# A float64 piece's conversion in the empty places of a weight tile's scale chain

## The chip, the cores and the metric

One core of a Trainium2 chip runs the kernel. The metric is the device time of one execution in microseconds, lower is better; it is given as the median of several runs.

## The reference

Attention with a sliding window of 128 keys and a distance bias gives x (2304 tokens, 512 wide). A mixture of experts follows: `P` comes from eight rounds of row and column normalisation of `exp(x @ w_gate)`, and the output is the sum over eight experts. A last block has a leaky ReLU:

```python
for e in range(E):                       # E = 8, D = 512, F = 1024
    h = np.maximum(x @ w1[e], 0.0)
    out += P[:, e:e + 1] * (h @ w2[e])
...
h = x @ w_in                             # 512 x 2048, float64 here
g = np.maximum(0.01 * h, h)
return (g @ w_out).astype(np.float32)    # 2048 x 512, float64 here
```

`w_in` and `w_out` arrive as float64; all other inputs are float32.

## The kernel before

After the attention the two feed-forward blocks are worked through in 20 **chunks** of 512 hidden columns: 16 for the experts (two for each), four for the last block. A chunk has a first weight tile (512 x 512 of `w1` or `w_in`) and a second one (512 x 512 of `w2` or `w_out`). The tokens stand in five groups, `PAIRS` 0 to 4, of four or two tiles of 128; a **unit** is one chunk with one group, and from chunk 1 on the units of a chunk run in the order 0, 4, 1, 2, 3.

The 2 x 2 block products are formed with seven multiplications (`PRODUCTS`), each on operands split into two float16 halves, so that a product of 256 columns takes six matmuls. `a_steps` makes the seven products of the first multiplication for a unit (line 727), `b_steps` those of the second (line 844). A group of tokens with two halves has 14 a steps and 14 b steps, group 4 has 7 and 7; 126 steps make a chunk. Every product is taken out of PSUM by ACT or DVE before a later one adds to the same bank: a steps by ACT (L739, at the seventh product L751) or DVE (L743), b steps by DVE (L857) or by ACT and POOL (L854, L855). `later` hangs the ReLU, the split of h and its sums (L775, L781, L797 on ACT, L756 on DVE, L800 on POOL) some steps behind. `merge` weaves a unit's a steps with the b steps of the unit before.

Beside this runs the preparation of the next chunk's weights, in the list `side`. At unit 4 of a chunk `side_jobs` fills it; every step ends with a tick that takes the next one or two places of the list, a place being a job or `None`, an empty place. `Weights.load` brings 1 MB to a buffer `raw` (L571, on SP's queue). `Weights.scale` has four squares with a row sum (`largest`, L575, ACT), the eight places of `scale_jobs` (`one` L413 and L415 on DVE; `two` a matmul L421 and small DVE steps L423 to L434; `three` a matmul L440 and a copy L441; the other five are empty), then four scalings (L578, ACT). `early` has two splits (L446 on ACT, L447 on POOL) and four sums (L602, POOL); the other splits come with the last steps of the chunk, and only then is `raw` free. `W[0]` are the first weights (`a` in `side_jobs`), `W[1]` the second (`b`).

`to_single` turns a piece of 256 KB of `w_in` or `w_out` into float32 in DRAM. Its load (L650, 512 KB, SP) goes to a buffer `raw` too, and its five jobs are `exponent` (L656 on DVE, L659 on ACT), `signed` (L662, DVE), `high` (L667 on DVE, L668 on ACT), `low` (L674 on ACT, L676 on POOL) and `put` (L680 on POOL, then the store L681 on SP's queue). There are 32 pieces; chunks 1 to 10 convert three each, chunk 11 two, later ones none. `raw` has two buffers, so in a chunk with three pieces the first weights follow the first piece in one buffer, and the third piece and then the second weights follow the second piece in the other: each of these loads waits for the store of the piece whose buffer it takes, and SP's queue is in order.

What sets the order on each engine: the program is traced in the order in which the jobs are written, and `TileContext(nc, schedule_with_timeline_sim=True)` (L1100) orders each engine's queue when the kernel is compiled, from modelled times; of two instructions that it takes for ready the one written first goes first. `pop` ties every instruction of a job behind the last step instruction (`anchor`) of the same engine, and behind nothing else. So a place in the list is the earliest point of a job in its engine's queue.

Of the kernel before, what the change touches and what calls it, by code (L numbers as in the profile page):

```python
# [31 lines left out]
def attn_moe_kernel(  # L32
# [19 lines left out]
    KT = DM // P  # L52
# [577 lines left out]
    def weights(ci):  # L630
        for which in range(2):
            W[which][ci] = Weights(ci, which)
# [367 lines left out]
    def side_jobs(ci, n):  # L1000

        todo = [to_single(cast.pop(0)) for _ in range(min(n, len(cast)))]
        weights(ci)
        a, b = W[0][ci], W[1][ci]
        jobs = [load for load, _ in todo[:2]]
        if not todo:
            return [a.load, b.load] + [None] * 10 + a.scale() + a.early() + b.scale() + b.early()
        jobs += [None] * 8 + todo[0][1] + [a.load]
        if len(todo) > 1:
            jobs += todo[1][1]  # L1010
        if len(todo) > 2:
            jobs += [todo[2][0]] + [None] * 4 + a.scale() + todo[2][1] + [b.load] + a.early()
        else:
            jobs += [b.load] + [None] * 8 + a.scale() + a.early()
        return jobs + [None] * 8 + b.scale() + b.early()

    def weigh(ci):
        pu[ci] = small.tile([P, NTILE], F32, tag="pu", name="pu")
# [12 lines left out]
    for n, u in enumerate(units + [None]):  # L1031
        a, b = [], b_steps(*prev)
        if u is not None:
            ci, p = u
            assert ci < NCE or p in split_pairs
            a = a_steps(ci, p)
            k0 = len(a) - 7
            if p == ends[ci] and ci + 1 < NC:
                a = [[f] + ([lambda j=k - k0: W[0][ci + 1].at(j)] if k >= k0 else []) for k, f in enumerate(a)]
            else:  # L1040
                a = [[f] for f in a]
        if prev[1] == ends[prev[0]] and prev[0] + 1 < NC:
            k0 = len(b) - 7
            b = [[f] + ([lambda j=k - k0: W[1][prev[0] + 1].at(j)] if k >= k0 else []) for k, f in enumerate(b)]
        else:
            b = [[f] for f in b]
        if u is not None and ci >= 1:
            if n and units[n - 1][0] != ci and ci != NCE:
                weigh(ci)
            if p == 4:  # L1050
                side += side_jobs(ci + 1, 3 if ci < NCE - 1 else 0) if ci + 1 < NC else []
# [65 lines left out]
```

## Time and profile before

| | us |
|---|---|
| median of 3 runs | 1922.75 |
| lowest and highest of them | 1921.96, 1922.90 |
| the profiled execution | 1919.44 |
| its span, first to last instruction | 1917.6 |

| engine | busy us | share of the span |
|---|---|---|
| PE | 1846.7 | 96% |
| ACT | 1363.5 | 71% |
| POOL | 1325.3 | 69% |
| DVE | 1309.4 | 68% |

The profile is one execution on the core. Times are microseconds from the first instruction, unless ns is written. PE is TensorE's matmuls, DVE VectorE, ACT ScalarE, POOL GpSimd, SP the engine that issues all transfers; SPq marks an issue on its queue. L575 is line 575 of the kernel. An instruction is named by line, operation, and its tiles as out<-in. A row of a timeline has start, duration, engine, line, operation, tiles, shape, count, and in brackets the time for which the engine sat idle before it with what ended that idle time.

### The profile page before, as it was taken

What the parts mean: (1) busy time and instruction counts of PE and PEld (TensorE: products, weight loads), DVE (VectorE), ACT (ScalarE), POOL (GpSimd) and SP (SyncE); (2) the same over time, 40 slices, a digit from 0 to 9 for tenths busy, and PEclk for the clock granted to TensorE, in tenths of its full rate; (3) what the DMA queues carried; (4) which work ended last, traced back from release to release, by engine and by line L of the source; (5) the groups of instructions that cost most, each with busy time, mean ns of one, the idle gap of its engine ahead of it and who ended that gap; (6) DMA issues with size and microseconds to landing.
All of it is one profiled execution on the core that took longest, in us unless ns stands there. A gap on an engine that the chain in (4) does not pass through costs nothing.

```text
span 1917.6 us, 45101 instructions
## 1 busy us (share of the span) xinstructions
PE 1846.7 (96%) x17725; PEld 1606.4 (84%) x17725; DVE 1309.4 (68%) x3606; ACT 1363.5 (71%) x3125; POOL 1325.3 (69%) x1142
## 2 busy tenths in 40 slices
PE   7899889999999999999999999999999998999998
PEld 4677777888888888988888898988989787888897
DVE  5456567767676777767676777666666787677776
ACT  7978767776767677676676667666666779776764
POOL 3843566777868687877868687675767786665753
PEclk9999999999999999999999999999999999999999
DMA  7522002112111202111111201100001010101001
GB/s 231 171 89 84 2 19 77 33 63 64 43 57 39 84 24 72 51 45 67 40 62 34 84 23 56 45 23 23 23 24 45 1 46 1 45 2 45 2 29 72
DMA packets 57861, 97.80 MB, mean 51 GB/s; under 512 B 3632, under 2 KB 22064, under 8 KB 57648
## 3 DMA queue, kind: packets, MB, share of 16 engines
q1 hardware_dynamic: 57648, 94.92, 15.1%
q8 instruction: 138, 2.26, 0.5%
q14 instruction: 75, 0.61, 0.1%
HBM read 81.81 MB, written 13.11 MB: 49 GB/s over the span
## 4 chain that ended last, share of the span: by engine, by line
PE 76%; ACT 8%; DMA 5%; POOL 4%; DVE 4%; issue 2%; SPq 0%; POOLq 0%; ACTq 0%; DVEq 0%
PE t L844 36%; PE s L727 21%; PE sq L727 15%; DMA raw<-in_moe_w_dram 4%; ACT junk L575 2%; ACT e L261 1%; PE o L305 1%; DVE s L756 1%; POOL h L800 1%; PE pt L288 1%; PE s L249 1%; POOL w L447 1%; ACT xp L446 1%; ACT raw L578 1%; ACT pb L292 1%
## 5 line engine op out<-in xcount | busy, mean ns | idle before, releaser
L844 PE MATMUL t<-w,h 128*128 128x256 f16 x7560 | 978.7, 273 | 17.7 <-DVE acc L857 6.2
L727 PEld LDWEIGHTS <-w 128*128 128x128 f16 x8400 | 758.4, 98 | 110.4 <-issue 28.7
L844 PEld LDWEIGHTS <-h 128*128 128x128 f16 x7560 | 729.2, 98 | 114.5 <-issue 27.2
L727 PE MATMUL s<-xp,w 128*128 128x256 f16 (+1 forms) x4872 | 610.9, 262 | 18.5 <-ACT q L751 11.6
L857 DVE SCALAR_TENSOR_TENSOR acc<-t,pu,acc 128x256 f32<-128x256 f32 x864 | 407.2, 478 | 213.5 <-PE t L844 162.6
L800 POOL TENSOR_TENSOR h<-s,h 128x1024 f16<-128x1024 f32 x180 | 388.5, 2158 | 122.7 <-ACT h L797 81.8
L727 PE MATMUL sq<-xp,w 128*128 128x256 f16 (+1 forms) x3528 | 451.9, 262 | 3.0 <-DVE s L756 2.6
L855 POOL TENSOR_TENSOR acc<-acc,part 128x256 f32<-128x256 f32 x324 | 235.5, 729 | 283.1 <-ACT part L854 252.9
L447 POOL TENSOR_TENSOR w<-raw,w 128x512 f16<-128x512 f32 x240 | 277.8, 1167 | 45.9 <-ACT w L446 45.5
L756 DVE SCALAR_TENSOR_TENSOR h<-sq,h 128x512 f16<-128x512 f32 (+1 forms) x352 | 192.4, 551 | 84.2 <-ACT h L781 49.4
L854 ACT ACTIVATE part<-t,pu 128x256 f32<-128x256 f32 x324 | 152.6, 471 | 110.0 <-PE t L844 101.7
L797 ACT ACTIVATE h<-s 128x1024 f16<-128x1024 f32 x180 | 189.7, 1054 | 43.2 <-DVE s L756 41.7
L743 DVE SCALAR_TENSOR_TENSOR sq<-sq,q 128x256 f32<-128x256 f32 x352 | 150.0, 427 | 62.5 <-PE sq L727 54.8
L739 ACT ACTIVATE q<-s 128x256 f32<-128x256 f32 x364 | 137.8, 380 | 71.7 <-PE s L727 59.1
L446 ACT ACTIVATE w<-raw 128x512 f16<-128x512 f32 x240 | 148.2, 628 | 8.4 <-PE t L844 6.0
L756 DVE SCALAR_TENSOR_TENSOR s<-sq,s 128x256 f32<-128x256 f32 x352 | 145.9, 414 | 2.1
L775 ACT ACTIVATE h<-sq 128x512 f16<-128x512 f32 x176 | 104.4, 593 | 55.4 <-PE t L844 30.4
L756 DVE SCALAR_TENSOR_TENSOR s<-sq,q 128x256 f32<-128x256 f32 x352 | 131.4, 414 | 13.5 <-ACT q L751 11.7
L743 DVE SCALAR_TENSOR_TENSOR sq<-s,q 128x256 f32<-128x256 f32 x176 | 75.3, 428 | 84.0 <-ACT q L739 78.9
L575 ACT ACTIVATE junk<-raw 128x512 bf16<-128x512 f32 x160 | 100.2, 627 | 44.8 <-DMA raw<-in_moe_w_dram 43.6
L781 ACT ACTIVATE h<-sq 128x256 f16<-128x256 f32 x176 | 66.7, 379 | 65.0 <-DVE sq L743 58.2
L578 ACT ACTIVATE raw<-raw,sr 128x512 f32<-128x512 f32 x160 | 102.4, 716 | 2.3 <-DVE sr L441 1.9
(142 smaller groups left out, 1702.6 us busy)
## 6 DMA issues: line engine op xcount, KB each, us to landing
raw<-in_moe_w_dram SPq DMA_DIRECT2D x32, 1024.0 KB, 5.2
k_t<-in_k_dram SPq DMA_DIRECT2D x16, 512.0 KB, 4.0
raw<-in_moe_w_in_dram SPq DMA_DIRECT2D x16, 512.0 KB, 3.6
raw<-in_moe_w_out_dram SPq DMA_DIRECT2D x16, 512.0 KB, 3.5
q_t<-in_q_dram SPq DMA_DIRECT2D x18, 256.0 KB, 4.1
v_t<-in_v_dram SPq DMA_DIRECT2D x18, 256.0 KB, 2.7
acc<-in_v_dram SPq DMA_DIRECT2D x18, 256.0 KB, 6.0
out_dram<-acc SPq DMA_DIRECT2D x18, 256.0 KB, 2.0
```

The costliest lines, as they stand in the source:

```text
L446: nc.scalar.activation(out=hi, in_=src, func=AF.Copy)
L447: return nc.gpsimd.tensor_tensor(out=lo, in0=src, in1=hi, op=ALU.subtract)
L575: nc.scalar.activation(out=junk, in_=self.raw[:, k], func=AF.Square, accum_out=self.mx[:, k:k + 1])
L727: nc.tensor.matmul(d[b][:, f, :], t[:, wp, kk, ft * P:(ft + 1) * P], XP[p][:, o, kk, xp, :], start=(i == 0 and f == 0 and j in FIRST), sto ...
L743: nc.vector.scalar_tensor_tensor(out=block(k), in0=ps, scalar=CS, in1=q[:, k], op0=ALU.mult, op1=ALU.add)
L756: nc.vector.scalar_tensor_tensor(out=out, in0=in0, scalar=sc, in1=in1, op0=op0, op1=op)
L797: nc.scalar.activation(out=h[:, 3:7, 0, :], in_=d["s"], func=AF.Copy)
L800: nc.gpsimd.tensor_tensor(out=h[:, 3:7, 1, :], in0=d["s"], in1=h[:, 3:7, 0, :], op=ALU.subtract)
L844: nc.tensor.matmul(ps, h[:, o, hp, f, tt * P:(tt + 1) * P], w[:, wp, ft, :], start=(i == 0 and j in FIRST), stop=(i == 5), skip_group_chec ...
L854: nc.scalar.activation(out=part, in_=ps, func=AF.Copy, scale=s)
L855: nc.gpsimd.tensor_tensor(out=dst, in0=dst, in1=part, op=ALU.add)
L857: nc.vector.scalar_tensor_tensor(out=dst, in0=ps, scalar=s, in1=dst, op0=ALU.mult, op1=ALU.add)
```

## The change

It alters `side_jobs` where three pieces are converted. The first weights' squares move eight places back, so that 18 places lie between their load and the first of them. The third piece's five conversion jobs leave their places behind the scalings and take the five empty places of the first weights' scale chain. The second weights' load moves one place forward, the first weights' scalings nine back (behind that load), and `early` three back; three empty places less stand ahead of the second weights' squares, which keep their place. The list keeps its 85 places. With two pieces or none the list is the same as before.

```diff
         jobs = [load for load, _ in todo[:2]]
         if not todo:
             return [a.load, b.load] + [None] * 10 + a.scale() + a.early() + b.scale() + b.early()
+        scale = a.scale()
         jobs += [None] * 8 + todo[0][1] + [a.load]
         if len(todo) > 1:
             jobs += todo[1][1]
         if len(todo) > 2:
-            jobs += [todo[2][0]] + [None] * 4 + a.scale() + todo[2][1] + [b.load] + a.early()
+            load, cast_jobs = todo[2]
+            cast_jobs = list(cast_jobs)
+            chain = [cast_jobs.pop(0) if job is None and cast_jobs else job for job in scale[KT:KT + 8]]
+            jobs += [load] + [None] * 12 + scale[:KT] + chain + cast_jobs + [b.load] + scale[KT + 8:] + a.early() + [None] * 5
         else:
-            jobs += [b.load] + [None] * 8 + a.scale() + a.early()
-        return jobs + [None] * 8 + b.scale() + b.early()
+            jobs += [b.load] + [None] * 8 + scale + a.early() + [None] * 8
+        return jobs + b.scale() + b.early()
```

Places of the list of 85, counted from 0:

| job | before | after |
|---|---|---|
| first weights' load | 15 | 15 |
| second piece's five jobs | 16 to 20 | 16 to 20 |
| third piece's load | 21 | 21 |
| first weights' squares | 26 to 29 | 34 to 37 |
| `one`, `two`, `three` | 30, 33, 36 | 38, 41, 44 |
| `exponent`, `signed`, `high`, `low`, `put` | 42, 43, 44, 45, 46 | 39, 40, 42, 43, 45 |
| second weights' load | 47 | 46 |
| first weights' scalings | 38 to 41 | 47 to 50 |
| first weights' splits and sums | 48 to 53 | 51 to 56 |
| second weights' squares | 62 to 65 | 62 to 65 |

## Rows read from the trace of the kernel before

**Rows 1.** The page's head: span, and busy time of each engine

```profile
span 1917.6 us, 45101 instructions
PE 1846.7 (96%) x17725; PEld 1606.4 (84%) x17725; DVE 1309.4 (68%) x3606; ACT 1363.5 (71%) x3125; POOL 1325.3 (69%) x1142
```

**Rows 2.** Busy time by stretch: PE, PEld, DVE, ACT, POOL, PEclk, DMA; chunks 9, 14

```profile
941.40:1026.60 85.20, 84.04 (x804) 74.49 (x803) 60.50 (x155) 59.89 (x130) 65.55 (x56) 1.00 0.16 54
1347.00:1430.60 83.60, 83.60 (x804) 74.62 (x803) 54.20 (x146) 54.45 (x121) 57.32 (x49) 1.00 0.08 27
```

**Rows 3.** Who waited for whom: us in total, times, longest us

```profile
ACT junk L575 <- DMA raw<-in_moe_w_dram: 43.6, 22, 2.8
...
PE s L727 <- ACT q L751: 11.6, 13, 1.5
```

**Rows 4.** Timeline of ACT in chunk 9, around the first weights' squares

```profile
976.23 0.38 ACT L751 ACTIVATE q<-s 128x256 f32<-128x256 f32 x1 [0.72 <-PE s L727]
...
982.10 0.60 ACT L775 ACTIVATE h<-sq 128x512 f16<-128x512 f32 x1 [0.50 <-DVE sq L743]
985.10 0.63 ACT L575 ACTIVATE junk<-raw 128x512 bf16<-128x512 f32 x1 [2.40 <-DMA raw<-in_moe_w_dram]
...
986.82 0.63 ACT L575 ACTIVATE junk<-raw 128x512 bf16<-128x512 f32 x1
...
987.45 0.36 ACT L781 ACTIVATE h<-sq 128x256 f16<-128x256 f32 x1
987.72 0.37 ACT L751 ACTIVATE q<-s 128x256 f32<-128x256 f32 x1
```

**Rows 5.** Timeline of PE in the same stretch

```profile
985.53 1.52 PE L844 MATMUL t<-w,h 128*128 128x256 f16 x12
988.14 1.70 PE L727 MATMUL s<-xp,w 128*128 128x256 f16 x12 [1.09 <-ACT q L751]
```

**Rows 6.** Timeline of SP in chunk 9: third piece's load, second weights' load

```profile
987.40 0.33 SPq L650 DMA_DIRECT2D raw<-in_moe_w_out_dram  x1
...
1005.83 0.38 SPq L571 DMA_DIRECT2D raw<-in_moe_w_dram  x1
```

**Rows 7.** DMA issues by line: count, KB each, median us from issue to landing

```profile
raw<-in_moe_w_out_dram SPq DMA_DIRECT2D x16, 512.0 KB, 3.5
```

**Rows 8.** Timeline of DVE in chunk 9: the third piece's steps

```profile
991.04 0.43 DVE L656 TENSOR_SCALAR raw<-raw 128x512 int32<-128x512 int32 x1
...
992.60 1.17 DVE L667 TENSOR_SCALAR raw<-raw 128x512 int32<-128x512 int32 x1
...
999.11 1.37 DVE L662 SCALAR_TENSOR_TENSOR raw<-raw,sign 128x512 int32<-128x512 int32 x1
```

**Rows 9.** Timeline of DVE in chunks 2 and 3: the third piece's first step

```profile
393.88 0.60 DVE L656 TENSOR_SCALAR raw<-raw 128x512 int32<-128x512 int32 x1 [2.31 <-DMA raw<-in_moe_w_in_dram]
...
480.78 0.43 DVE L656 TENSOR_SCALAR raw<-raw 128x512 int32<-128x512 int32 x1 [0.58 <-DMA raw<-in_moe_w_in_dram]
```

**Rows 10.** Timeline of PE in chunk 2, right after that step

```profile
394.87 0.71 PE L727 MATMUL s<-xp,w 128*128 128x256 f16 x5 [0.32 <-DVE sq L743]
...
398.28 0.82 PE L844 MATMUL t<-w,h 128*128 128x256 f16 x6 [1.07 <-ACT part L854]
```

**Rows 11.** Timeline of ACT in a chunk without pieces: the first square

```profile
1313.50 0.38 ACT L751 ACTIVATE q<-s 128x256 f32<-128x256 f32 x1
1313.76 0.63 ACT L575 ACTIVATE junk<-raw 128x512 bf16<-128x512 f32 x1
```

**Rows 12.** Timeline of POOL in chunk 9: the sums' split, the third piece's last product

```profile
991.35 2.13 POOL L800 TENSOR_TENSOR h<-s,h 128x1024 f16<-128x1024 f32 x1 [1.21 <-ACT h L797]
...
1002.43 1.27 POOL L680 TENSOR_TENSOR raw<-raw 128x512 f32<-128x512 f32 x1
```

**Rows 13.** Timeline of ACT in chunk 9: the second weights' first square

```profile
1011.06 0.63 ACT L575 ACTIVATE junk<-raw 128x512 bf16<-128x512 f32 x1 [1.66 <-DMA raw<-in_moe_w_dram]
```

## The prediction

> **What bounds the kernel now.** I read the page's busy times first: PE is busy for 96% of the span [rows 1], so time can come only from places where PE stands. Then the busy times by stretch, one chunk against another: a chunk with three float64 pieces takes 85.20 us for 804 matmuls, one without pieces 83.60 us for the same 804, at the same granted clock, full speed [rows 2]. There are ten chunks with three pieces (the change alters those alone), so at most about 10 x 1.6 = 16 us, 0.8%, stand in what the pieces cost PE. Third, the waits: ACT's squares L575 wait 43.6 us for raw weights, 22 times, and PE waits 11.6 us for ACT's L751 [rows 3]. The timelines of one chunk join the two. ACT is done with L775 at 982.70, its next instruction is the first square, and that starts at 985.10, when the 1 MB load has landed; L781 and L751 stand behind the squares and run at 987.45 and 987.72 [rows 4]. PE, which needs the bank that L751 empties, stands 1.09 us in the meantime and goes on at 988.14 [rows 5]. That one stop is most of the 1.6 us.
>
> **What limits the move.** A place in the list is one tick; the first 14 places go two to a step, the later ones one to a step, and a step is about 83.60 / 126 = 0.66 us [rows 2] (126 steps a chunk, counted in the code). The list is 85 long before and after. The first weights' squares go from places 26 to 29 to 34 to 37: eight steps, 5.3 us, against an ACT wait of 2.40 us. Read so, the wait would vanish. But a place is only a lower bound: a job is tied behind the latest step of its own engine, and the rest of the order is the compile-time plan's. Where the load came long ago, the first square stands right behind the L751 it is tied to, 1313.50 and 1313.76 [rows 11]. In a chunk with pieces the L751 that place 26 is tied to ran at 976.23, and the square stands 6 us further back, behind L775 [rows 4]: there not its place but the landing that the plan reckons with put it in the queue. The new places tie the first two squares behind unit 1's fourth product, whose copy L739 stands ahead of L775, so these two may stay exactly where they are, wait included. The third and fourth are now tied behind L751 itself; the fourth stood there already. So what I count on is one square: the third leaves L751's way.
>
> **The parts and their cost.**
> No work is added or removed: the same four squares, eight scale jobs, five conversion jobs, four scalings, two splits, four sums; three empty places less ahead of the second weights, whose squares keep place 62.
> Third square: from its start to L781's, 987.45 - 986.82 = 0.63 us [rows 4]. L751 comes that much sooner and PE's stop falls from 1.09 to about 0.46 [rows 5]. Bounds: 0, if the plan leaves this order; 1.09, if two squares or all go behind L751. I take 0.63, nearest to the row, in seven chunks (the fourth to the tenth load the squares in this order): 7 x 0.63 = 4.4 us. In the first three chunks the order around the squares differs and the next wait is nearer; I take 0 there, between -1 and +1 each.
> The third piece's first step, L656 on DVE, goes from place 42 to 39. This is where a gain can be lost: its load is issued at 987.40 [rows 6], behind the second piece's store, which nothing here moves; a piece of this kind lands 3.5 us after its issue [rows 7], so at 990.9, and L656 starts at 991.04 [rows 8]. It has no spare time. Whatever ACT gains ahead of it becomes a wait of DVE for that load, and behind L656 in DVE's queue stand the evictions L857 and L743 that PE needs. What such a wait costs PE can be read in the early chunks: 0.58 us at 480.78 [rows 9] is followed by no stop of PE, 2.31 us at 393.88 [rows 9] by stops of 0.32 and 1.07 [rows 10]. With L656 at the same spot in the queue the wait is the gain itself, 0.63: about nothing. Three places of its own do not move it, since its old and its new place are tied behind the same step on DVE (L743 of the eighth a step) and no DVE step lies between; bounds 0 to 1.4 us a chunk.
> Steps L667 and L662 of the piece: the old places tied them behind later DVE steps (L667 at 992.60, L662 at 999.11 [rows 8]); the new ones let them follow L656 at once. That puts up to 1.17 + 1.37 = 2.5 us of DVE work ahead of an eviction; PE has at least the 0.58 of rows 9 in hand and DVE gets the 1.37 back where L662 was. Bounds 0 to 1.0; I take 0, for no PE stop follows L667 where it is now.
> Store and second load: with L662 early, L680 no longer runs at 1002.43 behind L800 [rows 12] but about 2.5 us before; the store and the second weights' load (issued 1005.83 [rows 6], on SP's queue behind that store) come as much sooner, and the second squares' wait of 1.66 at 1011.06 [rows 13] shrinks. PE does not stand for that wait in the later chunks, so it gives little: 0 to 2 us in all, I take 0.5. L800 runs about 1.3 us later for it; its product is needed several steps on.
> The chain's later jobs (L423 to L441) and the scalings come up to nine places later, splits and sums three; the weights they make are for the next chunk: 0.
>
> **The sum.** 4.4 + 0.5 = 4.9 us. The profiled execution took 1919.44 us (span 1917.6 and 1.84 around it) and would take 1914.5; the median of the runs, 1922.75, lies 3.3 above it, so I forecast 1922.75 - 4.9 = 1917.9.
>
> **Rivals.**
> Nothing moves: the plan keeps the third square too, or DVE's wait for the third piece takes back what ACT gives. For it: L656 without spare time [rows 8]; against it: the tie behind L751. Time 1922.5, between 1919 and 1925.
> Everything vanishes: the squares pass the landing, DVE's order moves so that L656 comes after its load, and chunks run at 83.60: 10 x 1.6 and some 2 us at the second squares, 18 us, 1904.5. Against it: the load of the third piece is tied to the second piece's store, and nothing puts L656 later.
> Slower: L656, three places earlier, does go earlier in DVE's queue, by 3 x 0.66 = 2.0 us, and waits 0.63 + 2.0 = 2.6 us for its load. Rows 9 and 10 price that: (0.32 + 1.07) / 2.31 x 2.6 = 1.6 us of PE, less the 0.63, so 0.9 us in ten chunks, 9 us: 1932. It decides once the wait is above about 1 us, where 0.6 us of PE for each us of wait eats the 0.63. For it: the early chunk of 393.88; against it: the same tie on DVE.
>
> Held steps: L667 at 992.60 takes 1.17 us beside POOL's L800, which runs from 991.35 on, where L656, of the same shape, takes 0.43 [rows 8, 12]. In a row beside L800, L667 and L662 could hold an eviction back by the difference, 0.74 us, in ten chunks 7.4 us: 1925.3. Against it: no PE stop follows the long L667 now, and DVE is free of L662 later. The Trainium skill, SBUF — State Buffer, section Who interferes with whom, speaks for this case: a VectorE instruction with two SBUF inputs, or in a two-port mode, and a GpSimd instruction that reads SBUF keep each other from a shared port for a whole instruction. By that rule, which the long L667 fits, the held one would wait out L800 entirely, 2.13 us, rather than 0.74.
>
> **Chances.** The forecast 0.44, with a range of its own from 1912 to 1921; nothing moves 0.22; everything vanishes 0.10; slower 0.16; held steps 0.08. A difference under 0.2% (3.8 us) can't be told from no change here. Faster: 0.37 of the forecast's 0.44 and the whole of "everything vanishes", 0.47. Same: 0.06 of the forecast, 0.20 of "nothing moves", 0.05 of "held steps", 0.31. Slower: what is left, 0.22. The range reaches from 1908, short of "everything vanishes", to 1931, just short of the slower case's value; about 2 in 10 stay outside.
>
> **What would show it.** Right: in a late chunk the first square still waits for its load behind L775, the third stands behind L751, PE's stop for L751 is about 0.4 to 0.5, L656 waits some 0.6 us for the piece's load and PE does not stand behind it; L680 runs ahead of L800 and the second load is issued some 2 us sooner in its chunk; a chunk with pieces takes about 84.6. Wrong: squares without any wait (the plan did follow the places), or a wait of DVE at L656 above 1 us with PE stops at L743, L857 or L854 behind it, or PE stops at a new spot, such as the evictions beside L662.

## The result, and the profile after

| | before | after |
|---|---|---|
| median, us | 1922.36 | 1943.60 |
| lowest and highest, us | 1921.14, 1922.90 | 1943.29, 1943.72 |
| ratio, 95% interval | | 1.0115 (1.0103 to 1.0128) |
| the profiled execution's span, us | 1917.6 | 1941.5 |

The change makes the kernel 21 us slower; forecast were 4.9 us less. (The spans differ by 23.9: the profiled execution of before, 1919.44 us, lies 2.9 below its median, that of after, 1943.29, only 0.3.) The head of the page of after, which answers to [rows 1] (lines below `side_jobs` stand four further down in the kernel after; those above have the same numbers):

```profile
span 1941.5 us, 45062 instructions
PE 1860.8 (96%) x17725; PEld 1612.2 (83%) x17725; DVE 1313.3 (68%) x3606; ACT 1363.0 (70%) x3125; POOL 1325.1 (68%) x1142
```

The same work, and ACT, DVE and POOL as busy as before within 4 us. So the question is where PE stands. To cut the span into chunks I take the one ACT instruction that a chunk has in `weigh` (L1023 before, L1027 after), in chunks 2 to 15. It comes last in these groups by source line: count, shortest, median and longest in ns, then the first and the last start in us, before and after:

```profile
L1023 ACT ACTIVATE pu<-Pm,rw x14: 313/322/338, 342.2 to 1430.6; 128x18 f32<-128x18 f32 x14
```
```profile
L1027 ACT ACTIVATE pu<-Pm,rw x14: 310/328/342, 342.6 to 1440.4; 128x18 f32<-128x18 f32 x14
```

Busy time by stretch (columns as in [rows 2]): chunks 2 to 10, chunk 11, chunks 12 to 14, chunk 15 to the end; first before, then after:

```profile
342.20:1111.80 769.60, 757.10 (x7213) 670.07 (x7211) 543.95 (x1386) 542.92 (x1170) 589.61 (x496) 1.00 0.16 54
1111.80:1195.20 83.40, 83.40 (x802) 74.30 (x801) 59.18 (x153) 57.62 (x127) 62.61 (x54) 1.00 0.14 45
1195.20:1430.60 235.40, 235.40 (x2268) 210.00 (x2266) 152.71 (x413) 153.84 (x340) 161.48 (x139) 1.00 0.09 28
1430.60:1917.60 487.00, 467.13 (x4384) 408.90 (x4381) 354.30 (x937) 337.94 (x747) 317.11 (x262) 1.00 0.08 28
```
```profile
342.60:1120.50 777.90, 760.59 (x7214) 670.35 (x7213) 546.37 (x1387) 538.43 (x1173) 589.16 (x495) 1.00 0.16 53
1120.50:1205.00 84.50, 83.96 (x805) 74.63 (x804) 58.53 (x153) 57.84 (x128) 63.03 (x55) 1.00 0.13 45
1205.00:1440.40 235.40, 235.40 (x2269) 209.93 (x2267) 155.45 (x412) 155.75 (x341) 161.78 (x140) 1.00 0.09 28
1440.40:1941.50 501.10, 473.09 (x4385) 411.10 (x4382) 354.96 (x938) 340.67 (x747) 316.82 (x262) 0.99 0.08 28
```

Read the first number behind the bounds. Of 23.9 us more, chunks 2 to 10, whose lists the change alters, have 8.3 and chunk 11 has 1.1; chunks 12 to 14 are equal; and 14.1 us arise from chunk 15 on, where the change alters no list and the same matmuls run.

In the changed chunks the forecast's own mechanism is there. ACT in chunk 9 of after, to be laid beside [rows 4]: the first square still stands behind L775 and waits for its load, and the third one now stands behind L751.

```profile
986.86 0.60 ACT L775 ACTIVATE h<-sq 128x512 f16<-128x512 f32 x1 [0.50 <-DVE sq L743]
990.25 0.63 ACT L575 ACTIVATE junk<-raw 128x512 bf16<-128x512 f32 x1 [2.79 <-DMA raw<-in_moe_w_dram]
...
992.11 0.38 ACT L751 ACTIVATE q<-s 128x256 f32<-128x256 f32 x1
992.38 0.63 ACT L575 ACTIVATE junk<-raw 128x512 bf16<-128x512 f32 x1
```

Then the third piece meets its load and POOL: DVE, POOL and PE in the same chunk. L656 waits 1.12 us, takes 1.90 for the 0.43 of [rows 8], and PE stops.

```profile
995.88 1.90 DVE L656 TENSOR_SCALAR raw<-raw 128x512 int32<-128x512 int32 x1 [1.12 <-DMA raw<-in_moe_w_out_dram]
```
```profile
995.37 2.13 POOL L800 TENSOR_TENSOR h<-s,h 128x1024 f16<-128x1024 f32 x1 [0.21 <-ACT h L797]
```
```profile
998.23 0.81 PE L844 MATMUL t<-w,h 128*128 128x256 f16 x6 [0.82 <-DVE acc L857]
```

PE's waits over chunks 3 to 10 (columns as in [rows 3]), before and after: less for L751, more for everything else. They hold 4.0 of the 7.4 us by which these chunks got longer; of the rest, 2.4 us is longer busy time of PE for the same matmuls (676.3 us for 673.9), which these views do not explain.

```profile
PE s L727 <- ACT q L751: 8.1, 8, 1.1
PE t L844 <- DVE acc L857: 0.4, 1, 0.4
PE t L844 <- ACT part L854: 0.4, 2, 0.2
```
```profile
PE t L844 <- DVE acc L857: 4.8, 10, 0.8
PE s L727 <- ACT q L751: 4.2, 9, 1.1
PE t L844 <- ACT part L854: 2.5, 6, 0.7
PE sq L727 <- DVE s L756: 1.7, 2, 0.9
```

### The profile page after: what moved, and what is told of

The parts are those of the page before. It is cut to its first block, busy times and chain, and to the rows that moved or that the text cites. A ratio compares the mean times of both kernels' runs of the same rounds, so it can differ in the third digit from the quotient of the medians.

```text
span 1941.5 us, 45062 instructions
## 1 busy us (share of the span) xinstructions
PE 1860.8 (96%) x17725; PEld 1612.2 (83%) x17725; DVE 1313.3 (68%) x3606; ACT 1363.0 (70%) x3125; POOL 1325.1 (68%) x1142
## 4 chain that ended last, share of the span: by engine, by line
PE 65%; ACT 12%; DVE 8%; DMA 6%; POOL 4%; issue 3%; SPq 0%; POOLq 0%; ACTq 0%; DVEq 0%
PE t L844 31%; PE s L727 18%; PE sq L727 13%; DMA raw<-in_moe_w_dram 4%; ACT junk L575 2%; DVE acc L857 2%; DVE h L756 2%; DVE s L756 1%; ACT e L261 1%; ACT raw L578 1%; DVE sq L743 1%; PE o L305 1%; ACT h L797 1%; PE pt L288 1%; PE s L249 1%
## 5 line engine op out<-in xcount | busy, mean ns | idle before, releaser
L844 PE MATMUL t<-w,h 128*128 128x256 f16 x7560 | 980.9, 273 | 33.9 <-DVE acc L857 14.2
L844 PEld LDWEIGHTS <-h 128*128 128x128 f16 x7560 | 730.5, 98 | 136.3 <-issue 44.3
L857 DVE SCALAR_TENSOR_TENSOR acc<-t,pu,acc 128x256 f32<-128x256 f32 x864 | 407.7, 478 | 201.9 <-PE t L844 151.1
L800 POOL TENSOR_TENSOR h<-s,h 128x1024 f16<-128x1024 f32 x180 | 384.1, 2134 | 127.0 <-ACT h L797 96.8
L727 PE MATMUL sq<-xp,w 128*128 128x256 f16 (+1 forms) x3528 | 444.5, 262 | 4.1 <-DVE s L756 3.6
L854 ACT ACTIVATE part<-t,pu 128x256 f32<-128x256 f32 x324 | 152.6, 471 | 97.8 <-PE t L844 92.2
L743 DVE SCALAR_TENSOR_TENSOR sq<-sq,q 128x256 f32<-128x256 f32 x352 | 150.3, 428 | 89.6 <-PE sq L727 78.3
L743 DVE SCALAR_TENSOR_TENSOR sq<-s,q 128x256 f32<-128x256 f32 x176 | 75.5, 429 | 98.9 <-ACT q L739 90.9
L775 ACT ACTIVATE h<-sq 128x512 f16<-128x512 f32 x176 | 104.4, 593 | 37.2 <-PE t L844 14.4
L578 ACT ACTIVATE raw<-raw,sr 128x512 f32<-128x512 f32 x160 | 102.3, 713 | 3.0 <-DVE sr L441 2.7
L781 ACT ACTIVATE h<-sq 128x256 f16<-128x256 f32 x176 | 67.0, 381 | 52.6 <-DVE sq L743 47.4
```

The lines of the kernel that those rows point to most:

```text
L727: nc.tensor.matmul(d[b][:, f, :], t[:, wp, kk, ft * P:(ft + 1) * P], XP[p][:, o, kk, xp, :], start=(i == 0 and f == 0 and j in FIRST), sto ...
L743: nc.vector.scalar_tensor_tensor(out=block(k), in0=ps, scalar=CS, in1=q[:, k], op0=ALU.mult, op1=ALU.add)
L800: nc.gpsimd.tensor_tensor(out=h[:, 3:7, 1, :], in0=d["s"], in1=h[:, 3:7, 0, :], op=ALU.subtract)
L844: nc.tensor.matmul(ps, h[:, o, hp, f, tt * P:(tt + 1) * P], w[:, wp, ft, :], start=(i == 0 and j in FIRST), stop=(i == 5), skip_group_chec ...
L854: nc.scalar.activation(out=part, in_=ps, func=AF.Copy, scale=s)
L857: nc.vector.scalar_tensor_tensor(out=dst, in0=ps, scalar=s, in1=dst, op0=ALU.mult, op1=ALU.add)
```

## Experiments

Two theories for the 14.1 us at the end. A: the compile-time plan orders all that follows anew once something ahead has moved, and the order at which it arrives behind the changed chunks is a worse one. B: the edit's own cost is carried over on the chip. The compiled queues depend on single empty places: with one place less in the list of chunk 12, the kernel after has the last sixth of its queues in the order of the kernel before (some 2950 matmuls, with what the other engines do beside them); with one less in that of chunk 15, the kernel before has the last tenth in the order of the kernel after (1964 matmuls). The traces of e1 and e2 show these orders. This table has all runs; the stretches are from the profiled execution of each, the ratio is against runs of the kernel before on the same chip.

| run | median us | ratio (95%) | chunks 2 to 10 | 12 to the end |
|---|---|---|---|---|
| before | 1922.36 | | 769.6 | 722.4 |
| after | 1943.60 | 1.0115 (1.0103 to 1.0128) | 777.9 | 736.5 |
| e1 | 1930.56 | 1.0048 (1.0033 to 1.0063) | 779.8 | 722.8 |
| e2 | 1935.65 | 1.0075 (1.0058 to 1.0092) | 770.7 | 736.7 |
| e3 | 1925.54 | 1.0020 (1.0011 to 1.0029) | 775.9 | 722.4 |
| e4 | 1924.76 | 1.0015 (1.0006 to 1.0025) | 771.6 | 722.4 |
| e5 | 1928.04 | 1.0036 (1.0023 to 1.0049) | 776.0 | 722.4 |
| e6 | 1928.39 | 1.0038 (1.0023 to 1.0053) | 774.7 | 723.3 |
| e7 | 1924.13 | 1.0015 (1.0006 to 1.0024) | 773.8 | 723.3 |
| e8 | 1923.55 | 1.0010 (1.0001 to 1.0020) | 772.3 | 722.4 |
| e9 | 1934.25 | 1.0065 (1.0049 to 1.0081) | 782.3 | 723.5 |
| e10 | 1940.21 | 1.0096 (1.0074 to 1.0118) | 788.8 | 723.3 |
| e11 | 1921.56 | 1.0001 (0.9991 to 1.0010) | 769.4 | 724.1 |
| e12 | 1919.87 | 0.9992 (0.9983 to 1.0002) | 769.6 | 720.7 |
| e13 | 1928.17 | 1.0036 (1.0023 to 1.0049) | 775.1 | 722.4 |
| e14 | 1927.29 | 1.0032 (1.0020 to 1.0045) | 775.3 | 723.4 |
| e15 | 1921.08 | 0.9997 (0.9988 to 1.0006) | 769.9 | 723.0 |
| e16 | 1921.39 | 1.0001 (0.9992 to 1.0011) | 769.9 | 723.2 |
| e17 | 1928.50 | 1.0039 (1.0025 to 1.0053) | 776.0 | 722.4 |
| e18 | 1929.60 | 1.0046 (1.0029 to 1.0064) | 777.8 | 722.4 |

### The end: the changed chunks with the old tail, and the reverse

e1 edits the kernel after, e2 the kernel before (there `ci == 16`); `ci` is the chunk whose weights the list prepares, one more than the chunk that runs.

```diff
         if not todo:
-            return [a.load, b.load] + [None] * 10 + a.scale() + ...
+            return [a.load, b.load] + [None] * (9 if ci == 13 else 10) + a.scale() + ...
```

> The changed kernel, with one empty place less (9 for 10) in the list of chunk 12, which converts nothing and which the change does not touch. That place gives the instruction queues of chunks 14 to 19 the order that they have in the kernel before; chunks 1 to 11 keep the order of the changed kernel. Theory A (order handed on: some 14 us of the loss lie in the stretch from chunk 15 to the end, 487.0 us before and 501.1 after, and come from the order that the compile-time plan arrives at there, not from anything that the edit costs): that stretch goes back to 487.0, chunks 2 to 10 still take 777.9 us for 769.7, and the time is 1943.6 - 14.1 = 1929.5, between 1927 and 1932. Theory B (the edit itself costs all of it, and the last chunks are late through something carried over on the chip): the time stays within 3 us of 1943.6.

> The kernel before, with one empty place less (9 for 10) in the list of chunk 15, that is after the last conversion. Chunks 1 to 14 keep the order of the kernel before; the order from chunk 15 on is another one, and its last tenth is that of the changed kernel. Nothing of the change is in it. Theory A (order handed on): the stretch from chunk 15 to the end takes between 492 and 503 us for 487.0, so 1928 to 1938. Theory B (the edit itself): one empty place among 77 is worth nothing, 1922.4 within 3 us.

Both came out as theory A has it. With the whole change in, and one empty place taken out of a list that it does not touch, chunk 12 to the end takes 722.8 us for 736.5, and the kernel gains 13.0 us. With nothing of the change in, the other place brings 736.7. PE's stops in the last tenth are the same ones: here in after and in e2, each with 0.86, 1.11 and 1.15 us, and none of the three in before.

```profile
1798.39 0.82 PE L844 MATMUL t<-w,h 128*128 128x256 f16 x6 [0.86 <-ACT part L854]
1800.32 1.36 PE L844 MATMUL t<-w,h 128*128 128x256 f16 x11 [1.11 <-DVE acc L857]
...
1929.18 0.50 PE L844 MATMUL t<-w,h 128*128 128x256 f16 x3 [1.15 <-POOL h L800]
```
```profile
1791.57 0.82 PE L844 MATMUL t<-w,h 128*128 128x256 f16 x6 [0.86 <-ACT part L854]
1793.50 1.36 PE L844 MATMUL t<-w,h 128*128 128x256 f16 x11 [1.11 <-DVE acc L857]
...
1922.35 0.50 PE L844 MATMUL t<-w,h 128*128 128x256 f16 x3 [1.15 <-POOL h L800]
```

The last 1964 matmuls, which after and e2 have in one order and which ran at full clock in all three, can be set side by side (columns as in [rows 2]; before, after, e2):

```profile
1702.40:1917.60 215.20, 208.18 (x1967) 184.39 (x1964) 160.35 (x409) 135.57 (x296) 130.72 (x113) 1.00 0.09 33
```
```profile
1717.00:1941.50 224.50, 210.70 (x1967) 184.21 (x1964) 159.22 (x403) 136.51 (x298) 130.30 (x112) 1.00 0.09 32
```
```profile
1710.20:1934.40 224.20, 210.68 (x1966) 184.22 (x1964) 159.15 (x403) 136.40 (x298) 129.30 (x111) 1.00 0.09 32
```

So 9 of the 14 us lie there, by the order of the queues alone: e1, e12, e15 and e16, with the order of before, take 215.2 us for these matmuls too.

What an order does is seen at the longest stop of after, ahead of that stretch. ACT's four scalings L578 take 2.56 us; before, two evictions L851 stand ahead of them, after, L851 stands behind them and PE waits 2.85 us. ACT before, then ACT and PE after:

```profile
1618.91 0.47 ACT L851 ACTIVATE acc<-t,pu 128x256 f32<-128x256 f32 x1
1619.26 2.56 ACT L578 ACTIVATE raw<-raw,sr 128x512 f32<-128x512 f32 x4
```
```profile
1629.00 2.56 ACT L578 ACTIVATE raw<-raw,sr 128x512 f32<-128x512 f32 x4
...
1632.24 0.82 ACT L851 ACTIVATE acc<-t,pu 128x256 f32<-128x256 f32 x2
```
```profile
1632.75 1.44 PE L844 MATMUL t<-w,h 128*128 128x256 f16 x6 [2.85 <-ACT acc L851]
```

Is the 722.4 of the kernel before a lucky order, then? Four more kernels of before with another number of empty places in one later list (11 for chunk 12, 8 for 15, 12 for 14, 12 for 15):

> The kernel before with 11 empty places for 10 in the list of chunk 12. Nothing of the change. Chunks 1 to 11 have the old order; chunks 13 to 15 have in part the order of the changed kernel, the last three twentieths of the queues that of the kernel before. Theory A: the stretch from chunk 15 to the end lies between the 487.0 of the one order and the 501.2 of the other, and the half clock shows only if a long stop of PE does. If the order of the last chunks made no difference: 487.0 and 1921.

> The kernel before with 8 empty places for 10 in the list of chunk 15. Nothing of the change. The queues differ from those of the kernel before over about a tenth of their length, chunks 15 and 16, and are the same again behind. Theory A: the stretch from chunk 15 to the end is another number, between 480 and 500, by what stops PE has there; the stops from 350 us into the stretch on are those of the kernel before (0.3 to 0.6 us each, from 469 on). If the order of the last chunks made no difference: 487.0 and 1921.

> The kernel before with 12 empty places for 10 in the list of chunk 14. Nothing of the change. The queues differ from those of the kernel before over chunks 15 and 16. [...]

> The kernel before with 12 empty places for 10 in the list of chunk 15. Nothing of the change. As the run before it in the call: near 487 (484 to 490) if the order of the kernel before is an ordinary one, near 500 if it is a lucky one.

From chunk 12 on they took 724.1, 720.7, 723.0 and 723.2 (I count from chunk 12, since in e11 and e15 the `weigh` that marks the later chunks has itself moved). But by the traces all four come back to the queues of before 120 to 160 us behind the start of chunk 15 (of 487): their last 2950 matmuls take 329.4 to 329.8 us as before (329.8), where after and e2 need 342.3 and 341.5. So they draw a new order for the first third of the stretch only, and there that of before is an ordinary one (1.7 us more to 1.7 less). For the last two thirds the runs hold two orders, that of before and the slower one that after and e2 share at the end; whether before is lucky there stays open. That a neutral edit can produce the slow one is shown by e2. Differences of about 1 us between these sums are not all order: see the clock in the last section. The best of them, e12, is 0.9992 of before, and its interval includes 1: no kernel here beats the one before beyond doubt.

### The changed chunks: copies of the edit that stand alone

```diff
-        if len(todo) > 2:
+        if len(todo) > 2 and ci <= 9:        # e3: chunks 1 to 8
+        if len(todo) > 2 and ci == 11:       # e4: chunk 10
+        if len(todo) > 2 and ci in (5, 8, 11):   # e5: chunks 4, 7, 10
```

> The change in chunks 1 to 8 alone; chunks 9 and 10 keep the old list. From chunk 11 on every queue has the order of the kernel before. Theory A: the stretch from chunk 15 to the end takes 487.0 as before, chunks 2 to 8 take together about as much as in the changed kernel (602.1 us from 429.4 less 0.4... read from start of chunk 3 to start of chunk 9: 515.3 us after, 513.4 before), so the loss is 2 to 5 us and the time 1924 to 1928. Theory B: eight tenths of 21.2 us, 1939.

> The change in chunk 10 alone; from chunk 13 on and up to chunk 9 every queue has the order of the kernel before. What this measures is the edit by itself. Theory A: chunks 10 to 12 together within 2 us of the 238.7 us that they take before, and the time within 2 us of 1922.4. Theory B: a tenth of 21.2 us in that chunk, 1924.5. A third reading, my forecast before the run: 0.63 us less, 1921.7.

> The whole change, but in chunks 4, 7 and 10 alone; one chunk later each time, and from chunk 13 to the end, every queue has the order of the kernel before, so that three copies of the edit stand by themselves. In the kernel before the changed chunk and the next take 171.90 (chunks 4 and 5), 170.26 (7 and 8) and 168.58 us (10 and 11). With the change in chunk 10 alone the last pair took 171.06, 2.5 us more. If that is what the edit costs by itself: 2.5 us in each pair, 7.4 in all. If it was the luck of one place: pairs of either sign, and a sum within 3 us of nothing. My forecast before the first run: -0.6 in each.

e3 agrees with theory A: the old tail, and 6.3 us more in chunks 2 to 10 (515.4 us in chunks 3 to 8; theory B had 1939 us for the kernel). e4 does not: chunks 10 and 11 take 171.06 us for 168.58, more than the 2 us that theory A leaves to a single copy, so the edit also has a price of its own (by the number, 1924.76 us, e4 fits theory B's 1924.5). For the noise: in before, e2, e11, e12, e15 and e16, whose queues are the same up to chunk 11, such a pair of chunks varies by 0.5 to 0.8 us. In e5 chunks 4 and 5, 7 and 8, 10 and 11 take 174.45, 172.46 and 171.69 us for 171.90, 170.26 and 168.58: 2.5, 2.2 and 3.1 more, some 1.6 of it in the changed chunk and the rest in the next. All three copies have the same stops: for L751 46 us into the chunk, 0.32 to 0.34 where it was 1.02 to 1.09 (the gain); for L854 56 us in, 0.68; for L751 again, behind the second squares, 0.89 to 1.50. Here chunk 4 of e5 on DVE and POOL, then chunk 10 on DVE, POOL, ACT and PE:

```profile
564.49 1.48 DVE L656 TENSOR_SCALAR raw<-raw 128x512 int32<-128x512 int32 x1
```
```profile
563.54 2.14 POOL L800 TENSOR_TENSOR h<-s,h 128x1024 f16<-128x1024 f32 x1 [0.40 <-ACT h L797]
```
```profile
1082.41 1.06 DVE L656 TENSOR_SCALAR raw<-raw 128x512 int32<-128x512 int32 x1 [0.43 <-DMA raw<-in_moe_w_out_dram]
```
```profile
1081.05 2.13 POOL L800 TENSOR_TENSOR h<-s,h 128x1024 f16<-128x1024 f32 x1 [0.41 <-ACT h L797]
```
```profile
1087.07 0.38 ACT L781 ACTIVATE h<-sq 128x256 f16<-128x256 f32 x1 [1.48 <-DVE sq L743]
1087.35 0.47 ACT L854 ACTIVATE part<-t,pu 128x256 f32<-128x256 f32 x1
```
```profile
1078.03 1.70 PE L727 MATMUL s<-xp,w 128*128 128x256 f16 x12 [0.32 <-ACT q L751]
...
1087.87 0.82 PE L844 MATMUL t<-w,h 128*128 128x256 f16 x6 [0.68 <-ACT part L854]
...
1106.16 1.47 PE L727 MATMUL s<-xp,w 128*128 128x256 f16 x12 [0.89 <-ACT q L751]
```

Follow it: PE is 0.8 us ahead, and L800 starts about 1 us earlier in the chunk (48.9 to 49.1 us into it, before 49.8 to 50.2), while L656 starts 0.1 to 0.7 us later (49.8 to 50.2, before 49.5 to 49.9). So L656, which started ahead of L800, now starts behind it and is held to its end: 1.48, 1.58 and 1.06 us in chunks 4, 7 and 10 for the 0.43 of [rows 8]. It is not the wait for the load: chunks 4 and 7 have none (0.01 us at most) and the same stop of 0.68; the 0.43 of chunk 10 goes with a load that took 4.2 us for some 3.5, and L656 ends at the same place behind L800. Behind L656 DVE runs without a gap, and L667 and L662 (0.42 and 0.74 us, not held) stand in that row, up to the L743 that L781 waits for; L854, behind L781 on ACT, is what PE stands for.

Halves of the edit, and a move that has nothing to do with it, in the same three chunks:

```diff
# e6: squares at 34 to 37, the third piece at 42, 43, 45, 46, 47
+            jobs += [load] + [None] * 12 + s[:8] + c[:2] + [s[10]] + c[2:] + [b.load] + s[12:] + a.early()
# e7: squares at 26 to 29, the third piece at 39, 40, 42, 43, 45
+            jobs += [load] + [None] * 4 + s[:12] + [None] + c[:2] + [None] + c[2:4] + [None] + c[4:] + [b.load] + s[12:] + a.early()
# e8: the old list, 7 empty places for 8 ahead of b.scale()
```

> In the same three chunks only the first half of the change: the first weights' squares move eight places back, the third piece's first step keeps place 42 and its last goes from 46 to 47. If the squares' move is a gain and the conversion in the chain is what costs (the long L656 beside POOL's L800, L659 behind it, PE's stop at L854): PE's stop of 1.1 us for L751 is gone and nothing stands in its place, each pair of chunks 0.6 to 1.1 us shorter than before. If the squares' move itself costs (the chain and the scalings are later, so all that hangs on them is): each pair 1 to 2.5 us longer.

> In the same three chunks only the second half: the third piece's steps at places 39 to 45 and the second weights' load at 46 as in the change, the scalings behind it, the squares where they were (26 to 29). If the conversion is what costs: PE still stops 1.1 us for L751 and new stops of 0.7 us or more come beside L656, L667 and L662, each pair 1.5 to 2.5 us longer than before. If the squares' move is what costs: within 0.5 us of before.

> Nothing of the change. In the same three chunks one empty place less (7 for 8) stands ahead of the second weights' squares. This measures what any small move costs by the order alone. If the order of a chunk is as good as drawn anew by any move: pairs between 1 us shorter and 2.5 us longer than before, of either sign. If a move costs only what it moves: within 0.5 us of before in each pair.

(e6 and e7 are not clean halves: in both the scalings move behind the second weights' load as well, and in e6 that load moves one place back.) More per copy, as a mean over the three pairs: whole 2.6, squares alone 1.8, piece alone 1.1, one empty place 0.9. In e6 the changed chunk itself is 0.1 to 0.5 us longer: the gain at L751 is there (0.27 to 0.34 for 1.09 in two copies), and 0.99 us at L854 eats it, with L656 at its old place in the list but held behind L800 there too (1.55 and 1.13 us), and with L667 and L662 behind the L743s that matter; so the squares' move alone brings the meeting about. The chunk behind, whose list is the old one, is 1.1 to 2.0 us longer. e6 came out by its second reading (each pair 1.6 to 2.0 longer), e7 by neither (0.7, 0.6 and 2.1): neither half is the harmless one, and even the neutral move costs 0.7 to 1.1 us in each of its copies. In e7, whose copies have one order, it is a matter of tenths: in chunk 7 L656 starts 0.38 us ahead of L800, takes 0.42, and PE has no new stop (L662 is the one held, 2.04 us); in chunks 4 and 10 it waits 0.55 and 0.64 us for its load, starts 0.25 and 0.33 us behind L800's start, takes 2.16 and 2.07, and PE stops for 0.22 and then 0.57 or 0.58. The order of before repeats from chunk to chunk with one stop of about 1.1 us in each; each disturbance tried here put more stops there.

Can the piece be put out of L800's way?

```diff
# e9 (e10: one [None] more ahead of c, one less ahead of b.scale())
+            jobs += [load] + [None] * 12 + s[:12] + c + [b.load] + s[12:] + a.early()
# in both the second weights' squares stand at place 63 for 62
```

> In chunks 4, 7 and 10 the squares move as in the change, and the third piece's five steps go behind the scale chain, to places 46 to 50, instead of into it; the second weights' load follows at 51. Theory C (collision: what PE gains at L751 brings L656 ahead of its load and then beside POOL's L800, and PE pays for it at L854): here L656 comes after its load and not beside L800, so it waits for nothing and takes 0.43 us, PE's stop of 0.7 to 1.0 us some 55 us into the chunk is gone while the stop for L751 stays at 0.3, and the first 65 us of the three chunks are 0.7 us shorter than before each; behind that, the later store brings the second load 2 us later, and the second squares cost PE up to 1.5 us. Theory D (any order other than the one before costs about 1 us a copy): stops of the same sum at other spots, pairs 0.7 to 2.5 us longer.

> As the run before it in the call, with one more empty place: the third piece at places 47 to 51, the second weights' load at 52. Theory C: the same first 65 us of the three chunks, 0.7 us shorter than before each, without a stop at L854. Theory D: stops elsewhere again, with another sum.

In chunk 4 of e9 L656 comes long after its load and the stop 56 us in is gone, but PE stops 1.22 us for L751 and 0.87 and 0.91 at new spots, and the pairs are 3.3 to 3.9 longer. e10 is worse: 3.9 to 6.7 longer. The order moved once more, so theory C is not tested by these; of theory D, "elsewhere again" is seen, but its 0.7 to 2.5 us are passed by all six pairs.

### What holds L656

These four start from e5 and shorten a step of the same chunks. e13: L656 on 128 of 512 columns. e14: L680 on 128 columns. e17: an L800 on two of its four blocks with a memset for the rest; e18: on three.

> The kernel with the whole change in chunks 4, 7 and 10, and in the third piece of these chunks L656 works on 128 of the 512 columns; L659 behind it reads the loaded words in its place, so these three pieces come out wrong. The queues of ACT and POOL keep their order, DVE's one product L743 comes before L662 for after. If the long L656 beside L800 is what PE pays for at L854: L656 takes 0.2 to 0.3 us for 1.06, the stop of 0.68 is gone or below 0.1 in all three copies, and each changed chunk is 0.6 to 0.7 us shorter than with the whole step (87.47, 86.74, 86.63). If the wait for the load or the order is what PE pays for: the stop stays at 0.5 to 0.7.

> The kernel with the whole change in chunks 4, 7 and 10, and in these chunks the one L800 beside which the third piece's L656 runs takes two of its four blocks, a POOL memset clears the other two (these values come out wrong). In the stretch around L656 every queue keeps its order. L800 took 2.13 us from 1081.05 to 1083.18 in chunk 10 and L656 stood from 1082.41 to 1083.47. If L800 is what holds L656 and with it L743, L781 and L854: L800 takes about 1.1 us and ends before the third piece has landed, L656 takes 0.43, the stop of 0.68 falls by 0.6 to below 0.15 in all three copies, and each changed chunk is about 0.6 us shorter than 87.47, 86.74 and 86.63. If the order alone is the cause, or the wait for the load: the stop stays at 0.45 or above.

> As the run before it in the call, with three of the four blocks on L800 and a memset for the fourth: L800 takes 1.6 us for 2.13 and ends 0.5 us sooner. If L800 holds L656 to its own end: L656 ends about 0.5 us sooner and the stop of 0.68 falls to about 0.15 to 0.3, more than in the run with two blocks. If L800 is not the cause: 0.68 stays, as in the other.

The expected length of L656 in e13 was wrong by far. With a quarter of its columns it takes 1.37 us, and it ends at 1081.99, where POOL ends L800 (1079.78 + 2.13 = 1081.91). L656 is L657 and L800 is L801 in that kernel, a line further down:

```profile
1080.62 1.37 DVE L657 TENSOR_SCALAR raw<-raw 128x128 int32<-128x128 int32 x1
```
```profile
1079.78 2.13 POOL L801 TENSOR_TENSOR h<-s,h 128x1024 f16<-128x1024 f32 x1 [0.41 <-ACT h L798]
```

In e17 and e18 I shortened the wrong L800: L656 runs beside the one ahead of it, which stayed whole, and the memset, which depends on nothing, ran right behind this whole one. So POOL's work beside L656 became longer by 0.53 and 0.31 us, not shorter, and L656 went with it. e17, chunk 10:

```profile
1081.42 2.13 POOL L801 TENSOR_TENSOR h<-s,h 128x1024 f16<-128x1024 f32 x1 [0.40 <-ACT h L797]
1083.49 0.53 POOL L803 MEMSET h<- 128x512 f16 x1
```
```profile
1082.26 2.03 DVE L656 TENSOR_SCALAR raw<-raw 128x512 int32<-128x512 int32 x1
```

It ends at 1084.29, 0.27 behind the memset (1084.02). What PE pays follows it: in e13, e5, e18 and e17 L656 ends 0.08, 0.28, 0.53 and 0.74 us behind the end of the whole L800, in each of the three copies, and PE's stops at L844 within the next 6 us are 0.47, 0.68, 0.74 and 0.16 + 0.74, again in each copy. In chunk 10 of before L656 ends 2.07 ahead of L800's end, and there is no stop. L656 waited for its load in only two of these twelve copies (0.43 and 0.07 us). e5, e17 and e18 have one order around L656 but for the memset; in e13 one L743 stands behind L662 for ahead of it, and a product of PE elsewhere. That shows L656, held by POOL, as a cause of the stop. How much of the last 0.47 would be left with L656 free of L800 in the same order was not measured.

> The kernel with the whole change in chunks 4, 7 and 10, and in the third piece of these chunks L680 works on 128 of the 512 columns (these pieces come out wrong): the store behind it, and the second weights' load behind the store, are issued 0.9 us sooner. The queues keep their order but for the first of the second weights' squares, which the plan now puts ahead of L775. If PE's stop for L751 some 74 us into the chunk is the second load coming late: the squares wait 0.9 us less, and the stop of 1.50, 0.89 and 0.89 falls by 0.9 each, to about nothing in two copies. If the four squares in a row are what PE pays for, whenever the load comes: the stops stay within 0.3 of those.

The store came sooner, and the stops for L751 are 0.21 in all three copies, for 1.50, 0.89 and 0.89: they do hang on the second load. But the squares stand 2.04 us for it in chunk 10 with L775 behind the first one, PE stops 0.73, 0.33 and 0.25 at L844 in their place, and the three changed chunks gain only 0.05 to 0.24 us. By the size of the L751 stops the first reading holds, by the time neither does.

## Why the prediction was wrong, point by point

- **The third square.** Right. It stands behind L751, as [rows 4] with the tie of its place had it; the stop [rows 5] went from 1.02 to 1.09 down to 0.32 to 0.34 in the copies of e5, 0.68 to 0.77 for the 0.63 of the sum.
- **L656's wait taken as the gain itself, "about nothing".** The term was mis-sized. The wait was 0.01, 0.00 and 0.43 in the copies of e5 and 1.12 in chunk 9 of after, and in e5 it is not what PE paid for. What I did not price is that the gain brings L800 ahead of L656. Before, L656 ends (1076.59 in chunk 10) just as L800 starts (1076.52). My bound from [rows 9, 10] has this meeting only at its smallest: the L656 of 0.60 there started 1.8 us behind L800's start and was held for its last 0.3 us. In e5 it cost 0.68 us of PE, nearly the whole gain.
- **L667 and L662 in a row: 0, and the rival of held steps.** The rival had the mechanism and the wrong instruction. I priced it as 0.74 us on L667 from [rows 8, 12]; in e5 L667 and L662 are not held (0.42 and 0.74 us), and it struck L656, at up to the rest of L800. The Trainium skill, SBUF — State Buffer, section Who interferes with whom, says that a VectorE instruction in a two-port mode and a GpSimd one shut each other out for a whole instruction; the traces agree (L656 ends within 0.3 us behind POOL, whatever its columns). For L656 itself, the instruction held to the end of L800, the price by the rule was the better one; what PE paid for it, 0.68 us, is near the 0.74.
- **Store and second load about 2 us sooner.** Wrong in sign for copies that stand alone. In e5 the second load is issued 65.3 us into chunk 10, before 64.4; in chunks 3 to 10 of after it comes between 62.0 and 69.5, before 64.3 to 65.3. L676 no longer runs ahead of an L800 but behind it. L662's earlier place was not what set POOL's order.
- **The squares of the second weights.** Priced as 0.5 of gain; in e5 all four stand in a row ahead of L751, and PE stops 0.89 to 1.50 there.
- **All that the change does not touch: not in the sum at all.** The step that failed most. I wrote that the order is the compile-time plan's, and then counted seven chunks as if everything else kept its order and its 0. The 14.1 us from chunk 15 on are a plan's other order (e1, e2), and of the 2.6 us per copy a quarter to a half comes in the next chunk, with its old list. No rival had a price for it; the slower one I had (L656 earlier in DVE's queue) is not what happened.

So the sum failed in two places: L656's term, put at nothing, took the gain back in each copy (0.68 us), and the order of everything else, put at nothing without a reason, cost 14.1 us and more. Of 23.9 us of span: 14.1 the order at the end, shown by e1 and e2; 9.4 the changed chunks and chunk 11, of which copies standing alone show the parts; 0.4 ahead of chunk 2. In after the ten copies cost some 0.9 us each and not 2.6, in lengths that change from chunk to chunk (84.9 to 89.5 us), so neighbours do not add up. Which moved instruction makes the chunk behind a copy longer, why the order that after reaches behind chunk 12 costs time only from chunk 15 on, and why the plan comes to it at all, stays open.

## What to carry to other kernels

Where a planner orders the queues, an edit is priced on the whole compiled order: compare the queues behind the edit, and run a neutral edit of the same size beside it, so that an order's luck isn't taken for the edit's worth. Such a control speaks only for the stretch in which its queues differ, so look where they come together again. A step without spare time that is brought forward meets its load and then whatever runs there; look up what POOL does at the new time before calling the wait free. A gain that holds at its own stop (here 0.7 us) says little until the next two waits behind it are priced.

## What the runs showed of the hardware

- DVE's L656, L667 and L662, from SBUF to SBUF, are held when they start while a POOL instruction runs: in these traces L656 and L667 then end 0.28 us, L662 0.55 us behind its end. L656 took 0.59 to 2.16 us so, by what was left of the POOL instruction, and 1.37 with 128 columns (it ended 0.08 behind). Started 0.2 to 0.4 us ahead of L800, as in chunks 4 to 10 of before, it took 0.43. L800 is held as well: beside L662 it took 2.58 us for 2.13 (1085.05 in before). Evictions, which read PSUM (L743, L857), kept 0.4 to 0.5 us beside L800.
- TensorE's clock fell to its lower level at long stops that came in pairs: in after at 0.69 + 1.46 us and at 0.79 + 2.85 us, for some 3.4 and 6.8 us, with full load on PE from the end of the stop; in e2 and e11 at a pair of 0.7 and 1.46 us, for 3.4. Columns as above, PEclk the third from the end; 0.5 is 1.2 GHz:

```profile
1580.00:1584.00 4.00, 3.86 (x23) 2.85 (x24) 3.44 (x10) 2.59 (x5) 4.00 (x5) 0.57 0.00 0
1584.00:1590.00 6.00, 6.00 (x73) 5.57 (x71) 4.97 (x14) 3.31 (x7) 4.96 (x3) 1.00 0.26 84
...
1632.00:1639.00 7.00, 6.25 (x32) 4.68 (x32) 4.05 (x10) 6.03 (x12) 7.00 (x7) 0.54 0.00 0
```

The two stretches did 0.57 and 0.54 of the work that full speed gives: 3.86 x 0.43 + 6.25 x 0.46 = 4.5 us of work, by this estimate at most a third of the 14.1 (e2, which has the first stretch alone, is as slow). The same stops do not always bring the fall. In before a pair of 0.76 and 1.28 us (at 1589.6 and 1591.7) and a stop of 1.50 us (at 1623.23, for DVE) were followed by full clock, and so was that pair in e3 and e5; in e6, e7, e9, e10 and e14, with the same pair in the same order, 3.4 us at the lower level followed. PE and the stretch in e6:

```profile
1597.77 2.25 PE L844 MATMUL t<-w,h 128*128 128x256 f16 x12 [1.29 <-ACT acc L851]
```
```profile
1598.30:1601.70 3.40, 3.40 (x18) 2.62 (x17) 0.81 (x5) 2.32 (x5) 2.03 (x1) 0.50 0.02 5
```

In those five, chunk 12 to the end takes 723.3 to 723.5 us, and 722.4 in e3 and e5: 0.9 to 1.1 us for 3.4 us at the lower level, less than the 1.7 us of work it lost.
